# Chunked attention and four attention experts on one core: one written global order in place of four engine orders played out by a planner

## The chip, the cores and the metric

The kernel runs on one core of a Trainium2 chip. The metric is device microseconds of one launch; before the change the median of three runs is 378.93 us (377.97 to 379.02). The core has five engines with a queue of instructions each: TensorE (PE, matmuls; its weight loads are shown apart as PEld), VectorE (DVE), ScalarE (ACT), GpSimd (POOL) and SyncE (SP, which here only issues DMAs). Each engine works its queue in order; where an instruction needs another engine's result, or a buffer that another engine still reads, it waits and everything behind it on its engine waits with it.

## The reference, cut to what matters

```python
# q, k, v: (8, 8, 576, 64); chunks of 64 tokens
scores = scale * q_c @ k_c^T;  attn = softmax(scores)        # 64 x 64 per chunk and head
x = (attn @ v_c) as (8, 576, 512)                            # heads side by side
logits = x @ w_gate;  topk = two largest of four;  w = softmax over these two
for e in range(4):
    q, k, v = x @ wq[e], x @ wk[e], x @ wv[e]
    a = softmax(causal(scale * q @ k^T))                     # 576 x 576
    out += (e in topk) * w * (a @ v @ wo[e])
```

## The kernel before, in words

The 8 x 576 tokens are 36 groups of 128. `stage_a` does the chunked attention, for one group or two at once: loads of K, Q and V (L358, L359, L362, 256 KB each), QK (matmuls of 64 x 64, L468), row maxima, difference, exponential and sum (DVE L478, L480, L485; ACT L483), scaling on POOL (L496), a transpose (for the first five groups on PE, L369 with copies L505 on ACT; for all others POOL copy L376, DMA transpose L380, ACT copy L385), then the product with V (AV below, L541). Its result x is split in two float32r parts, high (ACT L554) and low (DVE L556). Weights are loaded (L412) and split in the same way (ACT L415, DVE or POOL L419).

For each batch b of 8 follow: projections to Q and K of the experts (`project_qk`, L584, 12 matmuls of 256 or 320 columns), to V and the gate's logits (`project_v`, L441), the gate (`gating`, 16 small POOL operations with two on DVE and one on ACT between), and for each of two pairs of experts `scores` (L679, mask and minimum on DVE L690, exponential on ACT L702), `weights` (scaling on POOL L724, transposes on PE L369 with ACT copies L744 and L748, the tallest block by POOL, DMA and ACT L385) and `values` (L773). `project_out` (L801, six matmuls of 512 columns) makes the output rows, copied by ACT or DVE (L806, L809) and stored by SP.

In the text a step is named by its function, batch and pair: "SC4.1" is `scores` of batch 4, pair 1; TR are the PE transposes of `weights`, VA is `values`, OUT is `project_out`, QK and AV are the two products of `stage_a` with the numbers of their groups.

Each step is added to a `Plan` as an operation with an engine, a duration, the operations it depends on and the buffers (`Slot`) it uses. `ORDER` holds for each engine the order of its operations as a list of numbers. `Plan.emit` plays the program out with the durations, `LAT` and `CHANGE` (the price of a change of matmul form on PE): an operation is written when its engine is free, its turn has come, its operands are there and a buffer is free; the buffer that came free first is taken (`u.t = u.pool.pop(0)`). Where PE had nothing ready before 25 us (`WARM`), the planner writes a warming matmul of 128 x 512 bf16 on the last free PSUM bank (L837); 43 of these stand in the built program, 40 have a record in the trace.

Of the kernel before, what the change touches and what calls it, by code (L numbers as in the profile page):

```python
# [36 lines left out]
def rows(i):  # L37
# [3 lines left out]
TICK = 3.4133  # L41
CHANGE = {("full", "quarters"): 0.158, ("full", "rows"): 0.135, ("full", "cols"): 0.170, ("quarters", "rows"): 0.153, ("quarters", "full"): 0.228,
          ("quarters", "cols"): 0.184, ("rows", "full"): 0.248, ("rows", "quarters"): 0.181, ("rows", "cols"): 0.204,
          ("cols", "full"): 0.205, ("cols", "quarters"): 0.161, ("cols", "rows"): 0.129}


START = {"PE": 0.9, "Pool": 6.0, "ACT": 2.5, "SP": 0.4}


# [11 lines left out]
class Op:  # L61
    __slots__ = ("eng", "dur", "fn", "deps", "uses", "rank", "at", "left", "after", "ready", "share", "form")


class Plan:


    LAT = {("PE", "PE"): 0.0, ("DVE", "ACT"): 0.13, ("ACT", "DVE"): 0.14, ("Pool", "PE"): 0.14, ("Pool", "DVE"): 0.13,
           ("DVE", "DVE"): 0.13, ("ACT", "ACT"): 0.13, ("Pool", "Pool"): 0.13, ("SP", "dma"): 0.0, ("dma", "load"): 2.0,
           ("dma", "turn"): 0.5, ("dma", "store"): 1.3}  # L70
# [4 lines left out]
    def add(self, eng, dur, fn, deps=(), uses=(), share=0.9, form="full"):  # L75

        o = Op()
        o.form = form
        o.eng, o.dur, o.fn, o.uses = eng, dur, fn, list(uses)
        o.deps = [d for d in deps if d is not None]  # L80
        o.share = share
        o.at = len(self.ops)
        o.after, o.ready, o.rank = [], 0.0, 0
        o.left = len(o.deps)
        for d in o.deps:
            d.after.append(o)
        for u in o.uses:
            u.left += 1
        self.ops.append(o)
        return o  # L90

    def emit(self, fill, until):

        free_at, avail = {}, {}
        cols, form, turn = {}, "full", {eng: 0 for eng in ORDER}

        def pe_time(dur, share, now):
            up = cols.get(int(now // TICK) - 1, 0.0) >= 0.375 * TICK
            dur = dur if up else 2.0 * dur
            t = now  # L100
            while t < now + dur - 1e-6:
                k = int(t / TICK + 1e-9)
                e = min(now + dur, (k + 1) * TICK)
                cols[k] = cols.get(k, 0.0) + (e - t) * share * (1.0 if up else 0.5)
                t = e
            return dur

        for eng, text in ORDER.items():
            own = [o for o in self.ops if o.eng == eng]
            for r, k in enumerate(text.split()):  # L110
                own[int(k)].rank = r
        for o in self.ops:
            avail.setdefault(o.eng, [])
            free_at.setdefault(o.eng, START.get(o.eng, 0.0))
            if o.left == 0:
                heapq.heappush(avail[o.eng], (o.rank, o.at, o))
        events = [(t, -1, None) for t in sorted(free_at.values())]
        now, left = 0.0, len(self.ops)
        while left:
            for eng, heap in avail.items():  # L120
                if free_at[eng] > now or not (heap or eng == "PE" and now < until):
                    continue
                back, got = [], None
                while heap:
                    item = heapq.heappop(heap)
                    o = item[2]
                    if o.rank != turn.get(eng, o.rank):
                        back.append(item)
                        break
                    need = {}  # L130
                    for u in o.uses:
                        if u.t is None:
                            need[id(u.pool)] = (u.pool, need.get(id(u.pool), (None, 0))[1] + 1)
                    if o.ready <= now and all(len(p) >= n for p, n in need.values()):
                        got = o
                        break
                    back.append(item)
                for item in back:
                    heapq.heappush(heap, item)
                if got is None:  # L140
                    if eng == "PE" and now < until:
                        fill()
                        free_at[eng] = now + pe_time(0.215, 1.0, now)
                        heapq.heappush(events, (free_at[eng], -1, None))
                    continue
                for u in got.uses:
                    if u.t is None:
                        u.t = u.pool.pop(0)
                got.fn()
                left -= 1  # L150
                dur = got.dur
                if eng == "PE":
                    dur = pe_time(dur + CHANGE.get((form, got.form), 0.0), got.share, now)
                    form = got.form
                if eng in turn:
                    turn[eng] += 1
                free_at[eng] = now + dur
                heapq.heappush(events, (now + dur, got.at, got))
            if not left:
                return max(free_at.values())  # L160
            assert events, "the plan is stuck"
            now = events[0][0] + 1e-9
            while events and events[0][0] <= now:
                o = heapq.heappop(events)[2]
                if o is None:
                    continue
                for u in o.uses:
                    u.left -= 1
                    if u.left == 0:
                        u.pool.append(u.t)  # L170
                for a in o.after:
                    a.left -= 1
                    a.ready = max(a.ready, now + self.LAT.get((o.eng, a.eng), 0.21))
                    if a.left == 0:
                        heapq.heappush(events, (a.ready, -1, None))
                        heapq.heappush(avail[a.eng], (now if a.eng == "dma" else a.rank, a.at, a))
# [10 lines left out]
def pool_t(n):  # L187
# [3 lines left out]
ORDER = {  # L191
    "PE": """
# [10 lines left out]
    """,  # L203
    "DVE": """
# [65 lines left out]
    """,  # L270
}
WARM = 25.0
TALL = (4,)
FIRST = 5
# [7 lines left out]
def chunked_attention_then_attention_experts(ctx: ExitStack, tc: tile.TileContext, qt, kt, vt, wqk, wvg, wo, out):  # L282
    nc = tc.nc
    pe, dve, act, pool = nc.tensor, nc.vector, nc.scalar, nc.gpsimd
# [592 lines left out]
```

## Time and profile before

| what | value |
|---|---|
| median of three runs | 378.93 us (377.97 to 379.02) |
| span of the profiled execution, first to last instruction | 376.5 us, 13435 instructions |
| around the span (median less span) | 2.4 us |
| busy: PE, ACT, DVE, POOL | 368.8, 302.5, 265.7, 245.9 us |
| chain that ended last, by engine | PE 79%, ACT 9%, DVE 3%, POOL 3%, DMA 2%, issue 2% |

The page gives busy times, a strip of 40 slices, the chain of work that ended last and the costliest groups. PE is busy nearly throughout, so an average says little; what counts are the few places where PE's queue stands still, and in the opening what it stands still for. PE's granted clock is shown as full in every slice of the strip. The records of matmuls overlap (they are pipelined), so a step's length is read from the start of its first matmul to the start of the next step's first.

### The profile page before, as it was taken

The numbers are of one execution on the slowest core, as the hardware profiler recorded it, in microseconds if no ns is written. First come the engines' busy times: TensorE is split into PE (matmuls) and PEld (weight loads), VectorE is DVE, ScalarE is ACT, GpSimd is POOL, SyncE is SP. The second block draws the span as 40 slices with busy tenths as digits, with TensorE's granted clock in tenths as the row PEclk, the third lists the DMA queues.
The fourth block names the chain that finished last, engine by engine and source line by source line (L and its number), as shares of the span: only waits on it lengthen the run. The fifth ranks groups of instructions, "written<-read, shape, count | busy, mean of one in ns | idle before, by whom it ended". The sixth has DMA issues, their size and how long they took to land.

```text
span 376.5 us, 13435 instructions
## 1 busy us (share of the span) xinstructions
PE 368.8 (98%) x5214; PEld 315.8 (84%) x5217; DVE 265.7 (71%) x895; ACT 302.5 (80%) x845; POOL 245.9 (65%) x447
## 2 busy tenths in 40 slices
PE   8999999999999999999999989999999999999996
PEld 3699889978889799887899789978898889976775
DVE  3769898679978943589697786867864675388631
ACT  2674899999987996898956989799985895799651
POOL 6571778996898059966774418999693039867700
PEclk9999999999999999999999999999999999999999
DMA  7968788589899803149799394669526002235634
GB/s 281 390 228 269 189 177 240 89 179 157 197 186 204 149 30 92 49 114 269 179 257 226 58 245 137 100 169 156 164 51 113 2 3 56 59 57 96 175 124 167
DMA packets 88624, 57.25 MB, mean 152 GB/s; under 512 B 68976, under 2 KB 69232, under 8 KB 88560
## 3 DMA queue, kind: packets, MB, share of 16 engines
q1 hardware_dynamic: 88416, 56.12, 60.3%
q8 instruction: 41, 0.67, 0.8%
q10 hardware_dynamic: 144, 0.26, 0.2%
q14 instruction: 23, 0.19, 0.2%
HBM read 30.42 MB, written 9.44 MB: 106 GB/s over the span
## 4 chain that ended last, share of the span: by engine, by line
PE 79%; ACT 9%; DVE 3%; POOL 3%; DMA 2%; issue 2%; SPq 0%; POOLq 0%; DVEq 0%; ACTq 0%
PE bank L584 21%; PE bank L801 14%; PE bank L441 11%; PE bank L773 11%; PE bank L679 8%; ACT at L702 5%; PE bank L468 4%; PE bank L369 4%; PE bank L541 4%; PE bank L837 3%; DMA wpT<-wp 1%; POOL at L724 1%; ACT et L385 1%; POOL en L496 1%; DMA qs<-in_qt_dram 1%
## 5 line engine op out<-in xcount | busy, mean ns | idle before, releaser
L724 POOL TENSOR_SCALAR at<-at,st,gate 128x192 f32<-128x192 f32 (+4 forms) x160 | 95.4, 609 | 11.9 <-DVE st L715 4.4
L702 ACT ACTIVATE at<-at,st 128x576 f32<-128x576 f32 (+4 forms) x160 | 89.8, 586 | 4.0 <-DVE st L690 3.8
L584 PE MATMUL bank<-xh,wqk_hi 128*128 128x256 f32 (+1 forms) x256 | 71.6, 302 | 0.0
L584 PE MATMUL bank<-xh,wqk_lo 128*128 128x256 f32 (+1 forms) x256 | 70.0, 296 | 0.0
L690 DVE CUSTOM_DVE_ANT_0 at<-bank,mask 128x320 f32<-128x320 f32 (+4 forms) x160 | 59.9, 422 | 14.0 <-PE bank L679 11.9
L496 POOL TENSOR_TENSOR en<-e,mx 128x512 f32<-128x512 f32 x36 | 37.6, 1058 | 27.1 <-DVE mx L487 24.1
L584 PEld LDWEIGHTS bank<-xh,wqk_hi 128*128 128x128 f32 x256 | 48.3, 189 | 2.3 <-issue 0.5
L584 PEld LDWEIGHTS bank<-xh,wqk_lo 128*128 128x128 f32 x256 | 48.4, 189 | 0.2
L773 PE MATMUL bank<-aT,vv 128*64 128x448 f32 (+4 forms) x384 | 47.0, 393 | 0.0
L584 PE MATMUL bank<-xl,wqk_hi 128*128 128x256 f32 (+1 forms) x256 | 44.5, 296 | 0.0
L773 PEld LDWEIGHTS bank<-aT,vv 128*64 128x64 f32 x384 | 24.6, 137 | 22.4 <-issue 15.7
L756 DVE STREAM_TRANSPOSE aT<-at 32x96 f32<-32x96 f32 x128 | 34.4, 269 | 11.7 <-POOL wp L376 3.7
L385 ACT ACTIVATE et<-wpT 128x1024 uint16<-128x1024 uint16 x31 | 36.9, 1192 | 6.1 <-DMA wpT<-wp 6.0
L748 ACT ACTIVATE aT<-bank 128x128 f32<-128x128 f32 (+1 forms) x160 | 37.2, 338 | 3.7 <-PE bank L369 3.5
L385 ACT ACTIVATE aT<-wpT 128x1024 uint16<-128x1024 uint16 x32 | 38.1, 1198 | 1.0 <-DMA wpT<-wp 0.8
L584 PEld LDWEIGHTS bank<-xl,wqk_hi 128*128 128x128 f32 x256 | 37.7, 189 | 0.0
L702 ACT ACTIVATION_READ_ACCUMULATOR at<-at,st 128x1 f32 (+1 forms) x160 | 35.9, 224 | 0.0
L376 POOL COPY wp<-at 128x1024 uint16<-128x1024 uint16 x32 | 32.8, 1036 | 1.0 <-DMA wpT<-wp 0.8
L441 PE MATMUL bank<-wvg_hi,xh 128*128 128x260 f32 x128 | 33.0, 289 | 0.0
L376 POOL COPY wp<-en 128x1024 uint16<-128x1024 uint16 x31 | 31.7, 1039 | 1.6 <-DMA wpT<-wp 1.3
L679 PE MATMUL bank<-kh,qh 64*128 64x288 f32 (+4 forms) x192 | 32.4, 325 | 0.1
L441 PE MATMUL bank<-wvg_lo,xh 128*128 128x260 f32 x128 | 32.2, 283 | 0.0
(104 smaller groups left out, 868.7 us busy)
## 6 DMA issues: line engine op xcount, KB each, us to landing
ks<-in_kt_dram SPq DMA_DIRECT2D x36, 256.0 KB, 4.3
vs<-in_vt_dram SPq DMA_DIRECT2D x36, 256.0 KB, 4.5
qs<-in_qt_dram SPq DMA_DIRECT2D x35, 256.0 KB, 4.6
out_dram<-y SPq DMA_DIRECT2D x35, 256.0 KB, 2.1
at<-in_wqk_dram SPq DMA_DIRECT2D x4, 256.0 KB, 6.5
wpT<-wp SPq DMA_TRANSPOSE x63, 3.4
at<-in_wvg_dram SPq DMA_DIRECT2D x2, 260.0 KB, 4.9
at<-in_wo_dram SPq DMA_DIRECT2D x2, 256.0 KB, 6.0
```

The lines of the kernel that those rows point to most:

```text
L376: pool.tensor_copy(p.t[:, :256 * n].rearrange("p (x n) -> p x n", x=2), src().bitcast(U16).rearrange("p (n x) -> p x n", x=2))
L385: act.activation(put().bitcast(U16).rearrange("p j (q x) -> p j q x", x=2), pt.t[:, :256 * n].rearrange("p (x j q) -> p j q x", x=2, j=n), ...
L441: pe.matmul(bk.t[0:rows, :W_VG], xp[:, k, cols], wp[:, k, :], start=(n == 0), stop=(n == 3 * KT - 1))
L496: pool.tensor_tensor(en.t.rearrange("p (s h k) -> p s h k", s=2, h=HP), ev, rv.to_broadcast([128, 2, HP, 64]), op=OP.mult)
L584: pe.matmul(bk.t[:, :c1 - c0], wp[:, k], xp[:, k, c0:c1], start=(n == 0), stop=(n == 3 * KT - 1))
L679: pe.matmul(bks[s].t[:rows(i), at:at + c1 - c0], q[own, cs], k[own, c0:c1], start=(x == 0), stop=(x == 2), skip_group_check=True)
L690: dve.tensor_tensor_reduce(out=a.t[:r, A_OFF[i] + c0:A_OFF[i] + c1], in0=bk.t[:r, at:at + w], in1=mask[:r, m0:m0 + w], scale=1.0, scalar=f ...
L702: act.activation(af, af, AF.Exp, scale=-1.0, bias=st.t[:r, 0, i, 0:1], accum_out=st.t[:r, 1, i, 0:1])
L724: pool.tensor_scalar(af, af, st.t[:r, 2, i, 0:1], gt.t[:r, i, e:e + 1], op0=OP.mult, op1=OP.mult)
L748: act.activation(dst, bk.t[:, s0:s0 + 64 * n].rearrange("p (j c) -> p j c", j=n), AF.Copy)
L773: pe.matmul(bk.t[64 * s:64 * s + 64, c0 - h0:h1 - h0], vs.t[:, j, 64 * (2 * pair + s):64 * (2 * pair + s) + 64], ts[s].t[:, 448 * j + c0:4 ...
L801: pe.matmul(bk.t[:, n0:n1], up[:, k, 128 * t:128 * t + 128], wp[:, k, n0:n1], start=(n == 0), stop=(n == 5), skip_group_check=True)
```

## The change

The same 2457 operations with the same matmuls, transfers and vector instructions are written in another order. `ORDER` is now one list over all engines; each number is an operation, and `w48` means eight warming matmuls into bank 4. `HOMES` gives the buffer number of each `Slot` in the order of the operations. `emit` no longer plays anything out: it writes the operations in the order of the list. The warming matmuls are 30 (8, 2, 15, 1 and 4, in five places) where the built program had 43.

```diff
-    def emit(self, fill, until):
-        free_at, avail = {}, {}
-        cols, form, turn = {}, "full", {eng: 0 for eng in ORDER}
...
-                if got is None:
-                    if eng == "PE" and now < until:
-                        fill()
-                        free_at[eng] = now + pe_time(0.215, 1.0, now)
...
-                for u in got.uses:
-                    if u.t is None:
-                        u.t = u.pool.pop(0)
-                got.fn()
...
+    def emit(self, fill):
+        homes = iter("".join(HOMES.split()))
         for o in self.ops:
+            for u in o.uses:
+                if u.t is None:
+                    u.home = int(next(homes))
+                    u.t = u.pool[u.home]
+        held, done = {}, set()
...
+        for k in ORDER.split():
+            if k[0] == "w":
+                for _ in range(int(k[2:])):
+                    fill(int(k[1]))
+                continue
+            o = self.ops[int(k)]
...
+            o.fn()
+            retire(o)
...
-ORDER = {
-    "PE": """
-3 0 9 4 1 6 2 5 57 61 12 10 7 55 63 53 13 8 11 16 14 58 64 18 60 62 59 73 15 75 76 20 74 56 54 17 68 66 67 65 90 24
...
-WARM = 25.0
+ORDER = """
+63 40 278 86 109 w48 69 66 20 70 25 72 w42 46 71 43 73 35 47 74 132 49 48 50 170 75 51 76 89 52 77 10 53 5 54 15 w615
...
-    plan.emit(lambda: banks and pe.matmul(banks[-1], warm[:, 0:128], warm, start=True, stop=True), WARM)
+    plan.emit(lambda i: pe.matmul(banks[i], warm[:, 0:128], warm, start=True, stop=True))
```

Three places of the built order follow; in the new one line numbers are lower by 50 from the function `load` on.

The first is SP's queue at the start of the program, before: ks and qs hold K and Q of a group, vs its V, and at a raw half of a weight.

```order
1 L358 DMA ks0_73<-in_kt_dram 128x512
2 L359 DMA qs0_69<-in_qt_dram 128x512
3 L412 DMA at0_107<-in_wvg_dram 128x520
4 L358 DMA ks1_74<-in_kt_dram 128x512
5 L358 DMA ks2_75<-in_kt_dram 128x512
6 L359 DMA qs2_71<-in_qt_dram 128x512
7 L358 DMA ks3_76<-in_kt_dram 128x512
8 L359 DMA qs3_72<-in_qt_dram 128x512
9 L362 DMA vs0_77<-in_vt_dram 128x512
10 L412 DMA at0_107<-in_wvg_dram 128x520
11 L362 DMA vs1_78<-in_vt_dram 128x512
12 L362 DMA vs2_79<-in_vt_dram 128x512
```

And the same stretch of SP's queue now.

```order
1 L308 DMA ks0_73<-in_kt_dram 128x512
2 L309 DMA qs0_69<-in_qt_dram 128x512
3 L308 DMA ks1_74<-in_kt_dram 128x512
4 L312 DMA vs0_77<-in_vt_dram 128x512
5 L308 DMA ks2_75<-in_kt_dram 128x512
6 L309 DMA qs2_71<-in_qt_dram 128x512
7 L308 DMA ks3_76<-in_kt_dram 128x512
8 L309 DMA qs3_72<-in_qt_dram 128x512
9 L312 DMA vs1_78<-in_vt_dram 128x512
10 L362 DMA at0_107<-in_wvg_dram 128x520 x2
11 L312 DMA vs2_79<-in_vt_dram 128x512
12 L362 DMA at1_108<-in_wo_dram 128x512
```

The second group's K (ks1) stands one place earlier, the V weights' first half seven places later with the second half behind it, and the load in fourth place is now the V of group 11, which is used much later.

The second place is POOL's queue in the gate of batch 1, before: gs and gw are the gate's scratch, wp the operand of a DMA transpose, en the scaled weights of `stage_a`.

```order
114 L496 TENSOR_TENSOR en_84<-e_81,mx_91 128x512
115 L376 COPY wp_114<-en_84 128x1024
116 L376 COPY wp_115<-at_108 128x1024
117 L376 COPY wp_113<-at_107 128x1024
118 L640 TENSOR_TENSOR gs_129<-gs_129 128x20
119 L641 TENSOR_TENSOR gs_129<-gs_129 128x5x2
120 L642 TENSOR_TENSOR gs_129<-gs_129 128x5
121 L643 TENSOR_SCALAR gs_129<-gs_129 128x5
122 L648 TENSOR_TENSOR gs_129<-gs_129 128x20
123 L649 COPY gate_127<-gs_129 64x16
```

And POOL's queue at the same gate now.

```order
113 L446 TENSOR_TENSOR en_84<-e_82,mx_92 128x512
114 L590 TENSOR_TENSOR gs_129<-gs_129 128x20
115 L591 TENSOR_TENSOR gs_129<-gs_129 128x5x2
116 L592 TENSOR_TENSOR gs_129<-gs_129 128x5
117 L593 TENSOR_SCALAR gs_129<-gs_129 128x5
118 L326 COPY wp_114<-en_84 128x1024
119 L326 COPY wp_115<-at_109 128x1024
120 L326 COPY wp_113<-at_107 128x1024
121 L598 TENSOR_TENSOR gs_129<-gs_129 128x20
122 L599 COPY gate_127<-gs_129 64x16
```

The sum (L643, now L593) and the scaling (L648, now L598) have a reciprocal on DVE between them; three copies now stand in that place instead of ahead of it.

The third place is PE ahead of the third group that two batches share (its `project_v` reads xch), before: the last products of SC4.1, then QK31, eight rows of two.

```order
1845 L679 MATMUL bank_62<-kh_102,ql_100 128x320
1846 L679 MATMUL bank_66<-kh_102,ql_100 128x320
1847 L468 MATMUL bank_61<-ks_73,qs_69 64x64 x2
1848 L468 MATMUL bank_64<-ks_73,qs_69 64x64 x2
1849 L468 MATMUL bank_61<-ks_73,qs_69 64x64 x2
1850 L468 MATMUL bank_64<-ks_73,qs_69 64x64 x2
```

And PE at that `project_v` now: the last products of AV23+24 run straight into it.

```order
1783 L491 MATMUL bank_62<-et_86,vs_79 64x64 x2
1784 L491 MATMUL bank_65<-et_86,vs_79 64x64 x2
1785 L391 MATMUL bank_66<-wvg_hi,xch_89 128x260
1786 L391 MATMUL bank_66<-wvg_lo,xch_89 128x260
1787 L391 MATMUL bank_66<-wvg_hi,xch_89 128x260
```

QK29+30 and QK31 have left the run AV25+26, AV23+24, QK29+30, SC4.1, QK31 and now stand ten steps later, behind a `project_qk` of batch 5.

## Rows read from the trace of the kernel before

**Rows 1.** The page's first part: busy us, share of the span, instructions.
```profile
PE 368.8 (98%) x5214; PEld 315.8 (84%) x5217; DVE 265.7 (71%) x895; ACT 302.5 (80%) x845; POOL 245.9 (65%) x447
```
**Rows 2.** Stretches: us, busy (x count) of PE, PEld, DVE, ACT, POOL; clock, DMA share, GB/s.
```profile
10.00:20.00 10.00, 9.68 (x184) 7.01 (x184) 7.65 (x21) 6.37 (x17) 6.14 (x6) 1.00 1.05 388
...
60.00:90.00 30.00, 29.75 (x468) 26.88 (x466) 23.03 (x80) 28.75 (x80) 26.00 (x48) 1.00 0.82 168
90.00:110.00 20.00, 19.98 (x319) 17.57 (x317) 17.21 (x56) 19.40 (x54) 18.66 (x27) 1.00 0.78 187
110.00:200.00 90.00, 89.99 (x1290) 77.42 (x1287) 66.86 (x227) 74.98 (x208) 59.95 (x103) 1.00 0.64 153
```
**Rows 3.** Timeline of PE, opening: start, us, engine, line, operation, count [idle before].
```profile
1.25 4.27 PE L837 MATMUL bank<-warm 128*128 128x512 bf16 x10 [1.25 <-DVE warm L319]
...
7.89 3.84 PE L837 MATMUL bank<-warm 128*128 128x512 bf16 x16
...
14.77 1.24 PE L541 MATMUL bank<-et,vs 64*64 64x64 f32 x64
16.17 1.46 PE L837 MATMUL bank<-warm 128*128 128x512 bf16 x6 [0.16 <-issue]
17.27 0.47 PE L441 MATMUL bank<-wvg_hi,xh 128*128 128x260 f32 x1
```
**Rows 4.** Timeline of SP's DMA issues, opening.
```profile
8.31 0.33 SPq L362 DMA_DIRECT2D vs<-in_vt_dram  x1
9.00 0.33 SPq L412 DMA_DIRECT2D at<-in_wqk_dram  x1
```
**Rows 5.** Timelines of DVE, ACT and POOL, opening.
```profile
8.02 0.76 DVE L478 TENSOR_REDUCE mx<-bank 128x4 f32<-128x256 f32 x2 [0.42 <-PE bank L468]
...
11.04 0.64 ACT L415 ACTIVATE wvg_hi<-at 128x520 fp32r<-128x520 f32 x1 [0.94 <-DMA at<-in_wvg_dram]
...
10.42 2.05 POOL L496 TENSOR_TENSOR en<-e,mx 128x512 f32<-128x512 f32 x2 [2.38 <-DVE mx L487]
```
**Rows 6.** DMA queues, whole span, then 211.9 to 224.3 us: packets, MB, share.
```profile
q8 instruction: 41, 0.67, 0.8%
...
q8 instruction: 1, 0.02, 0.5%
```
**Rows 7.** Timeline of PE around 219.55 us.
```profile
215.63 2.10 PE L541 MATMUL bank<-et,vs 64*64 64x64 f32 x128
217.54 1.11 PE L468 MATMUL bank<-ks,qs 64*64 64x64 f32 x64
...
219.55 0.32 PE L468 MATMUL bank<-ks,qs 64*64 64x64 f32 x2
221.20 0.69 PE L468 MATMUL bank<-ks,qs 64*64 64x64 f32 x30 [1.32 <-issue]
```
**Rows 8.** Timeline of PE, two waits for ACT's copies.
```profile
85.94 1.15 PE L541 MATMUL bank<-et,vs 64*64 64x64 f32 x60 [0.19 <-ACT aT L748]
...
345.95 0.50 PE L801 MATMUL bank<-wo_hi,uh 128*128 128x512 f32 x1 [0.61 <-ACT aT L748]
```
**Rows 9.** Timelines: POOL and PE at TR0, POOL at the gate, ACT and PE at VA0.1.
```profile
64.67 3.46 POOL L724 TENSOR_SCALAR at<-at,st,gate 128x192 f32<-128x192 f32 x6
69.69 1.09 PE L369 MATMUL bank<-ident,at 64*128 64x64 f32 x28
...
88.41 0.23 POOL L648 TENSOR_TENSOR gs<-gs 128x20 f32<-128x20 f32 x1 [2.56 <-DVE st L715]
...
92.40 1.16 ACT L385 ACTIVATE aT<-wpT 128x1024 uint16<-128x1024 uint16 x1
94.45 1.94 PE L773 MATMUL bank<-aT,vv 128*64 128x128 f32 x12
```
**Rows 10.** The chain that ended last, in order of time: start, us, what.
```profile
167.76 1.09 PE bank L468 x64
168.85 0.93 PE bank L541 x64
```

More of the change, by code (lines that the diff above doesn't have):

```diff
@@ L1 @@
 from contextlib import ExitStack
-import heapq
 import numpy as np
@@ L38, in rows @@
     return 128 if i else 64
[L41 to L47, printed above, removed]
 class Slot:
@@ L61 @@
 class Op:
-    __slots__ = ("eng", "dur", "fn", "deps", "uses", "rank", "at", "left", "after", "ready", "share", "form")
+    __slots__ = ("eng", "dur", "fn", "deps", "uses", "at", "after", "share", "form")
+NO_CODE = ("dma", "load", "turn", "store")
 class Plan:
-    LAT = {("PE", "PE"): 0.0, ("DVE", "ACT"): 0.13, ("ACT", "DVE"): 0.14, ("Pool", "PE"): 0.14, ("Pool", "DVE"): 0.13,
-           ("DVE", "DVE"): 0.13, ("ACT", "ACT"): 0.13, ("Pool", "Pool"): 0.13, ("SP", "dma"): 0.0, ("dma", "load"): 2.0,
-           ("dma", "turn"): 0.5, ("dma", "store"): 1.3}
     def __init__(self):
@@ L82, in add @@
         o.at = len(self.ops)
-        o.after, o.ready, o.rank = [], 0.0, 0
-        o.left = len(o.deps)
+        o.after = []
         for d in o.deps:
@@ L90, in add @@
         return o
-    def emit(self, fill, until):
-        free_at, avail = {}, {}
-        cols, form, turn = {}, "full", {eng: 0 for eng in ORDER}
[L97 to L111, printed above, removed]
-        for o in self.ops:
[L113 to L131, printed above, removed]
-                        if u.t is None:
[L133 to L139, printed above, removed]
-                if got is None:
-                    if eng == "PE" and now < until:
-                        fill()
-                        free_at[eng] = now + pe_time(0.215, 1.0, now)
-                        heapq.heappush(events, (free_at[eng], -1, None))
-                    continue
-                for u in got.uses:
-                    if u.t is None:
-                        u.t = u.pool.pop(0)
-                got.fn()
[L150 to L176, printed above, removed]
@@ new lines, in emit, with retire @@
+    def emit(self, fill):
+        homes = iter("".join(HOMES.split()))
+        for o in self.ops:
+            for u in o.uses:
[3 more added lines that the diff above has]
+        held, done = {}, set()
+        def retire(o):
+            done.add(o.at)
+            for u in o.uses:
+                u.left -= 1
+            for a in o.after:
+                if a.eng in NO_CODE and all(d.at in done for d in a.deps):
+                    retire(a)
+        for k in ORDER.split():
[4 more added lines that the diff above has]
+            o = self.ops[int(k)]
+            assert all(d.at in done for d in o.deps), "an operation before its operands"
+            for u in o.uses:
+                key = id(u.pool), u.home
+                assert held.get(key, u) is u or held[key].left == 0, "a buffer before it is free"
+                held[key] = u
+            o.fn()
+            retire(o)
+        assert len(done) == len(self.ops)
@@ L188, in pool_t @@
     return 0.24 + 0.833e-3 * n
-ORDER = {
-    "PE": """
[10 rows of a table removed]
-    """,
-    "DVE": """
[20 rows of a table removed]
-    """,
-    "ACT": """
[23 rows of a table removed]
-    """,
-    "Pool": """
[10 rows of a table removed]
-    """,
-    "SP": """
[6 rows of a table removed]
-    """,
-}
-WARM = 25.0
+ORDER = """
+63 40 278 86 109 w48 69 66 20 70 25 72 w42 46 71 43 73 35 47 74 132 49 48 50 170 75 51 76 89 52 77 10 53 5 54 15 w615
+115 23 30 78 118 207 28 116 24 55 119 92 80 117 0 57 56 93 164 29 38 95 w41 58 120 94 96 61 112 121 39 59 79 60 97 w04
[81 rows of a table added]
+"""
+HOMES = """
+3201112231111015700010100006741223231313712333245020265160012300017476003012221130511100003117100133232021222010020221
+0034513032210114600003315400122201007111016111311710000100022171020011122250332113521301021320461130012511021111203603
+3300002020302121157222410010024200501223332411310020120143300011000120203206022033112111302022047022211015130020111153
+0033402000212003013312233500020213204711000261110110100263406400101001557521233401436101141000605200021637152100032221
+7361140205271237365410073214133223675010007112607064012007152301201311201262311140703053654050616411413324576050111540
+2163520200162617310203202417512014230205765402151363261233700714101165200236370120274635101135110637311001120271014273
+6000562141332720661101110206360450120522730101123027427424140407177565061200244331136105271011512062200422007235040121
+4702152102406111016105317370403466413312005270121671012632622000173541002511070512020622241071520614052330331152461701
+21270272070722002470150121411035535071411202
+"""
 TALL = (4,)
```

149 rows, old and new, of the table ORDER are left out of this document.

## The prediction

> **What bounds the kernel now.** I read the busy times first, then the busy times by stretch, then the timeline of each engine where PE stands still. The reader is to see in the first that PE is busy for 368.8 of 376.5 us and no other engine for more than 302.5 [rows 1]: a new order can win only what PE stands still, plus what its own queue holds that isn't needed. The stretches say where that is. From 110 to 200 us PE is busy 89.99 of 90 us [rows 2], so nothing is to be had there. In the opening PE looks busy too (9.68 of 10 us between 10 and 20), but much of it is warming: ten warming matmuls from 1.25, sixteen from 7.89, six from 16.17, and the first projection only at 17.27 [rows 3]. In that stretch the DMA engines are full (share 1.05, 388 GB/s) [rows 2], SP's issues follow each other at 0.69 us (8.31 to 9.00) [rows 4], and a load of 256 KB at 388 GB/s takes 0.68 us. So the opening is bound by the sequence of loads and the chain DVE, ACT, POOL behind them, and PE fills it.
>
> Between 60 and 110 us a second engine is nearly full beside PE: ACT 28.75 of 30 and 19.40 of 20 us, POOL 18.66 of the last 20 [rows 2]. There PE's lead is small: the transposes TR0 start at 69.69 where POOL has finished their operands at 68.13, and VA0.1 starts at 94.45 where ACT's last copy for it ends at 93.56 [rows 9]. Later both have more room, and PE waits in only two visible places: 1.32 us inside QK31 [rows 7] and 0.61 us at 345.95 [rows 8].
>
> **The change part by part.** The sum is made against the profiled execution: a span of 376.5 us, and 2.4 us around it up to the median of 378.93.
>
> *The work itself.* Same matmuls, transfers and vector instructions. What differs on PE is how often its form changes (full, quarters, rows, columns): counted over the order without the warming matmuls 107 before, 109 now. A change costs 0.16 us: 64 matmuls of `stage_a` take 1.09 us behind another form and 0.93 behind their own [rows 10]. Two more are +0.3 us.
>
> *The warming matmuls.* Thirteen fewer than the 43 that were written. At full clock one is 0.22 to 0.24 us (16 in 3.84, six in 1.46), in the first 4.27 us 0.43 (ten) [rows 3]. Thirteen times 0.22 is 2.8 us of PE's queue, but they stood where PE waited anyway, so alone their removal is worth nothing; what counts is when the first projection can start.
>
> *The opening.* The chain to that projection goes: QK of groups 1 and 0, maxima and differences on DVE, exponential, sum, scaling on POOL, transpose, copy, AV, split of x, projection. Group 0's K is loaded one place earlier, which is 0.68 us; its first reduction on DVE at 8.02 had waited 0.42 for QK [rows 5] and now follows group 1's at once, so POOL's two scalings (10.42 to 12.47) [rows 5] and the transposes come some 0.4 us earlier. Both halves of the V weights now come at the place where the second stood; the second was split on ACT from 11.04 [rows 5], so the two are split from 11.0 to 12.3, and POOL's remainders (1.29 each) end at 14.7, ahead of need. ACT then copies group 0's transposes first and group 1's second half only after group 0's x is split. By these lengths AV0 starts at about 13.5 instead of 14.77 and the projection at 16.3 instead of 17.27. Against that the V of group 11 now stands fourth among the loads and puts all behind it 0.68 us back; that is in the times named. Behind the projection both orders run the same first steps; a wait of 0.3 us before a transpose at 26 us goes too. I take -1.0 us; bounds +0.7 (the load that isn't needed yet costs its whole length) and -2.8 (all thirteen matmuls).
>
> *The wait inside QK31.* PE stops at 219.87 after two of 32 matmuls of a step that has begun, so its operands are there; the profile shows no releaser ("issue") [rows 7]. One queue carries instructions in 41 transfers of 0.67 MB together [rows 6]; over PE's 5214 matmuls and 5217 weight loads [rows 1] that is 64 bytes each, so it is PE's program, about 256 instructions to a transfer. Between 211.9 and 224.3 us only one such transfer ran [rows 6], while PE worked off its densest run: 128 matmuls of AV from 215.63, 64 of QK, 12 of SC4.1 and two of QK31 [rows 7], each with its weight load, 412 instructions in 4.2 us. I read the wait as PE running out of program. The new order takes QK29+30 and QK31 out of that run. Counting in blocks of 256 from the start, PE before needed 3.3 us for the 320 instructions up to the place where it stopped and 4.3 or more at every other block; in the new order the least is 4.6. From the step's start to its resumption are 1.65 us, of which two matmuls and the change of form take about 0.15: I take -1.5 us; bounds 0 and -1.6.
>
> The Trainium skill, "Runtime: NRT & Kernel Launch", section "Instruction fetch mechanics", says that PE's program is fetched ahead in blocks of 256 instructions and that this is hidden, since dispatch is slower than the fetch. The block size agrees with the 0.67 MB in 41 transfers; that it is always hidden doesn't agree with the wait at 219.87, unless that has another cause. By the page this term would be 0 and the sum 1.5 us worse.
>
> *Waits on ACT between 85 and 90 us, at 120 and at 345.* At 85.94 AV11+12 stops after four matmuls for ACT's copies, and at 345.95 the first OUT of batch 5 waits 0.61 us [rows 8]. Measured from a step's first matmul to the next step's first, against the same steps elsewhere, these two cost 0.5 and 0.7 us, and two late starts of `scores` at 89 and 120 us cost 0.6 and 0.4: 2.2 us together. The new order puts AV11+12 behind SC1.1, and an OUT that is long ready between the transposes of batch 7. In the gate of batch 1 POOL had stood 2.56 us for a reciprocal on DVE [rows 9]; three copies now cover it, which gives the transposes of batch 1 more room. But in the same stretch ACT and POOL stay as full as they were. If PE comes to TR0 1.6 us earlier (0.6 by its place, 1.0 by the opening), POOL, whose operations up to there are the same in number and which finished 1.56 us ahead, must be earlier too. I take half, -1.1 us, bounds -2.2 and +2.
>
> *The end.* From VA7.1 on both orders hold the same steps, with one OUT more between VA7.1 and the last batch's; the last copies and stores are the same: 0, bounds -0.5 and +0.5.
>
> Sum: 0.3 - 1.0 - 1.5 - 1.1 + 0 = -3.3. With 376.5 and 2.4 this is 375.6; I say 375.8, since the opening's steps are the least sure.
>
> **The rivals.** *ACT and POOL take the lead back.* If they set the times from TR0 to VA1.0, what PE wins before 90 us is lost there, and only the refill and the wait at 345 remain: 0.3 - 1.5 - 0.6, or 377.1. For it speaks that ACT is at 96% there [rows 2]; against it that ACT's work ahead of VA0.1 is 1.5 us less in the new order, and that POOL's 2.56 us go.
>
> *The refill wait stays or moves.* In the new opening AV2, AV3, a transpose, QK5+6, QK7+8 and AV4 follow each other: 232 matmuls, in a stretch where the DMA engines are full. By its place between two transfers PE has 4.9 us there, against 3.3 where it stopped, but a transfer may be slower beside the loads. Then 1.5 us stay: 377.3.
>
> *Slower: transposes brought too near their scores.* Between the end of the `scores` of a pair and its first transpose lies a chain over DVE, ACT, DVE and POOL. In PE's own work the shortest such distance before was 15.1 us outside the last batch (batch 3, pair 0). Now it is 12.7 there, 15.4 instead of 18.0 at the first pair, and 16.4 and 20.7 instead of 31 and 36 at two others. If the chain needs what it had at the first two places, PE waits 2.4 + 2.6 = 5.0 us: 380.8. It decides from 4.3 us of such waits on. For it: ACT's 96%. Against it: 13.4 us was enough in batch 7, with no wait before its transposes, and from 110 us on ACT is busy 74.98 of 90 us only [rows 2].
>
> *The clock.* With fewer warming matmuls PE stands still in short pieces before 16 us. Its granted clock is full in all rows of the stretches. If it fell to 1.2 GHz and came back only some 4 us into the projections, they would take twice as long there, as the first warming matmuls do (0.43 against 0.22) [rows 3]: +4, or 379.8. No piece without work is longer than about 1 us by the times above, so I hold it for unlikely.
>
> **How the numbers follow.** Forecast 0.48, ACT and POOL 0.20, refill 0.12, transposes 0.10, clock 0.03, and 0.07 for more than forecast (all waits go and none comes: about 372.5). A measurement can't tell less than 0.3% (1.1 us: 377.8 to 380.1) from no change. The forecast ends below that nearly always; the second and third in two cases of three; the transposes and half of the clock cases lie above. That gives faster 0.72, same 0.16, slower 0.12. The forecast's own range is 373.6 to 377.5; the range over the cases is 372.9 to 379.0, with the transposes left out at its upper end.
>
> **What would show it.** The first `project_v` at about 16.3 us; the DMA share near 1 up to 24 us as before; no "issue" wait of over 1 us on PE; TR0 and VA0.1 1 to 2 us earlier than 69.69 and 94.45; POOL's first scaling at the gate of batch 1 without the wait of 2.56 us; the span 373 to 374 us. The forecast is wrong if PE waits for POOL or ACT at TR0, TR3 or VA0.1 by more than a microsecond, if a wait without releaser of that size stands at 24 to 28 us, or if the granted clock falls in the opening.

## The result, and the profile after

The changed kernel takes 383.04 us (median of 4 runs, 381.85 to 383.76), beside 378.51 us before (377.97 to 379.02): ratio 1.0111, interval 1.0078 to 1.0145. It is slower, where 375.8 was forecast.

The first part of the page after: busy us, share of the span (380.7 us), instructions.

```profile
PE 369.7 (97%) x5202; PEld 316.6 (83%) x5204; DVE 265.5 (70%) x895; ACT 301.4 (79%) x845; POOL 245.6 (65%) x447
```

Beside [rows 1] PE is busy 0.9 us longer, DVE, ACT and POOL a little less, and the span is 4.2 us longer. The chain that ended last does look different, before first, then after:

```profile
PE 79%; ACT 9%; DVE 3%; POOL 3%; DMA 2%; issue 2%; SPq 0%; POOLq 0%; DVEq 0%; ACTq 0%
```

```profile
PE 53%; DMA 14%; ACT 13%; POOL 8%; DVE 5%; issue 4%; SPq 2%; POOLq 0%; ACTq 0%; DVEq 0%
PE bank L534 13%; DMA wpT<-wp 12%; PE bank L751 10%; PE bank L391 8%; PE bank L723 8%; PE bank L629 6%; ACT at L652 4%; POOL at L674 4%; PE bank L418 3%; PE bank L491 3%; PE bank L319 2%; ACT aT L335 2%; POOL wp L326 2%; DMA qs<-in_qt_dram 2%; DVE at L640 2%
```

12% of the span, 46 us, now hangs on one kind of transfer, the transposes by DMA (wp to wpT). The stretches of [rows 2], after (line numbers after are 50 lower than before):

```profile
10.00:20.00 10.00, 8.82 (x217) 6.71 (x216) 7.69 (x22) 7.21 (x18) 8.45 (x8) 1.00 1.05 387
60.00:90.00 30.00, 29.23 (x407) 26.24 (x407) 23.16 (x78) 28.29 (x82) 25.71 (x46) 1.00 0.78 156
90.00:110.00 20.00, 19.97 (x395) 17.51 (x393) 15.50 (x54) 17.90 (x53) 14.48 (x20) 1.00 0.77 160
110.00:200.00 90.00, 87.26 (x1248) 74.93 (x1239) 66.59 (x222) 74.25 (x206) 59.77 (x104) 1.00 0.66 155
```

Where PE was busy 89.99 of 90 us before, it is busy 87.26. The clock is full in every stretch. Three places of PE's timeline answer to [rows 3, 7]: the first projection, QK7+8 and QK31.

```profile
16.41 0.39 PE L391 MATMUL bank<-wvg_hi,xh 128*128 128x260 f32 x1
...
26.98 1.09 PE L418 MATMUL bank<-ks,qs 64*64 64x64 f32 x59 [0.29 <-issue]
...
233.97 1.63 PE L418 MATMUL bank<-ks,qs 64*64 64x64 f32 x96
```

The projection starts 0.86 us earlier, and QK31 runs through. So what the change was read to bring is there. What it cost stands in the groups of instructions by line (busy, mean ns, idle time before them and its releaser), the two kinds of copies of transposed blocks, before and after:

```profile
L385 ACT ACTIVATE aT<-wpT 128x1024 uint16<-128x1024 uint16 x32 | 38.1, 1198 | 1.0 <-DMA wpT<-wp 0.8
...
L385 ACT ACTIVATE et<-wpT 128x1024 uint16<-128x1024 uint16 x31 | 36.9, 1192 | 6.1 <-DMA wpT<-wp 6.0
```

```profile
L335 ACT ACTIVATE aT<-wpT 128x1024 uint16<-128x1024 uint16 x32 | 38.4, 1208 | 6.4 <-DMA wpT<-wp 6.3
...
L335 ACT ACTIVATE et<-wpT 128x1024 uint16<-128x1024 uint16 x31 | 36.6, 1183 | 13.2 <-DMA wpT<-wp 13.0
```

ACT stands 19.3 us before such copies instead of 6.8. How that reaches PE is seen around 120 us, on ACT's timeline and then on PE's:

```profile
119.96 1.17 ACT L335 ACTIVATE aT<-wpT 128x1024 uint16<-128x1024 uint16 x1 [0.49 <-DMA wpT<-wp]
121.04 0.37 ACT L401 ACTIVATE vv<-bank 128x260 f32<-128x260 f32 x1
121.31 1.17 ACT L335 ACTIVATE aT<-wpT 128x1024 uint16<-128x1024 uint16 x1
122.37 0.38 ACT L401 ACTIVATE vv<-bank 128x260 f32<-128x260 f32 x1
```

```profile
120.97 0.40 PE L629 MATMUL bank<-kl,qh 64*128 64x288 f32 x2 [0.60 <-DVE kl L548]
...
122.80 0.24 PE L629 MATMUL bank<-kh,qh 64*64 64x64 f32 x1 [0.84 <-ACT vv L401]
```

The scores at 122.80 need a PSUM bank that a projection of V filled earlier. Its copy into vv (122.37) was ready, but stood on ACT behind two copies of transposed blocks (119.96, 121.31), the first waiting for its transfer. All eight banks are taken there. The row names vv; the cause stands two places ahead of it in ACT's queue.

From the first projection on, each step's length (first weight load to the next step's first) is compared with the lower quartile of like steps (same kind, same form of the next step); what is over counts as standing still:

| | before | after |
|---|---|---|
| first projection at | 17.25 | 16.41 |
| work of the steps | 343.27 | 344.04 |
| standing still | 11.53 | 15.73 |
| of it in QK31 (before), QK7+8 (after) | 1.64 | 0.52 |
| last step at | 372.05 | 376.18 |

Without those two stops, standing still grew from 9.9 to 15.2 us; 6.0 us of growth lies between 40 and 200 us, in a dozen waits of 0.3 to 1.0 us and smaller ones.

### The profile page after: what moved, and what is told of

Its sections match the earlier page's. It is cut to its first block, busy times and chain, and to the rows that moved or that the text cites. A ratio compares the mean times of both kernels' runs of the same rounds, so it can differ in the third digit from the quotient of the medians.

```text
span 380.7 us, 13403 instructions
## 1 busy us (share of the span) xinstructions
PE 369.7 (97%) x5202; PEld 316.6 (83%) x5204; DVE 265.5 (70%) x895; ACT 301.4 (79%) x845; POOL 245.6 (65%) x447
## 4 chain that ended last, share of the span: by engine, by line
PE 53%; DMA 14%; ACT 13%; POOL 8%; DVE 5%; issue 4%; SPq 2%; POOLq 0%; ACTq 0%; DVEq 0%
PE bank L534 13%; DMA wpT<-wp 12%; PE bank L751 10%; PE bank L391 8%; PE bank L723 8%; PE bank L629 6%; ACT at L652 4%; POOL at L674 4%; PE bank L418 3%; PE bank L491 3%; PE bank L319 2%; ACT aT L335 2%; POOL wp L326 2%; DMA qs<-in_qt_dram 2%; DVE at L640 2%
## 5 line engine op out<-in xcount | busy, mean ns | idle before, releaser
L674 POOL TENSOR_SCALAR at<-at,st,gate 128x448 f32<-128x448 f32 (+4 forms) x160 | 95.3, 611 | 18.0 <-DVE st L665 7.3
L534 PE MATMUL bank<-xh,wqk_hi 128*128 128x320 f32 (+1 forms) x256 | 71.8, 302 | 0.5 <-DVE st L640 0.5
L534 PE MATMUL bank<-xh,wqk_lo 128*128 128x320 f32 (+1 forms) x256 | 70.0, 296 | 0.0
L534 PE MATMUL bank<-xl,wqk_hi 128*128 128x320 f32 (+1 forms) x256 | 44.5, 296 | 0.0
L629 PE MATMUL bank<-kh,qh 64*128 64x288 f32 (+4 forms) x192 | 34.2, 326 | 2.1 <-ACT vv L401 0.8
L652 ACT ACTIVATION_READ_ACCUMULATOR at<-at,st 128x1 f32 (+1 forms) x160 | 32.9, 206 | 0.0
```

Of the source, the lines that this page charges most:

```text
L534: pe.matmul(bk.t[:, :c1 - c0], wp[:, k], xp[:, k, c0:c1], start=(n == 0), stop=(n == 3 * KT - 1))
L629: pe.matmul(bks[s].t[:rows(i), at:at + c1 - c0], q[own, cs], k[own, c0:c1], start=(x == 0), stop=(x == 2), skip_group_check=True)
L652: act.activation(af, af, AF.Exp, scale=-1.0, bias=st.t[:r, 0, i, 0:1], accum_out=st.t[:r, 1, i, 0:1])
L674: pool.tensor_scalar(af, af, st.t[:r, 2, i, 0:1], gt.t[:r, i, e:e + 1], op0=OP.mult, op1=OP.mult)
```

## The experiments

Each was timed beside the kernel before, which took 378.2 to 378.6 us. Times are medians, the ratio is to before, with its interval. Differences to the changed kernel are to its 383.04 us; its own interval (1.0078 to 1.0145) is 2.5 us wide, so a difference to it of a microsecond or two is at the edge of what can be told. Orders are shown by rows of the engine's program.

**Ready work passes waiting copies (ACT alone).** One place of 16:

```diff
+L401 ACTIVATE vv_105<-bank_65 128x260
+L401 ACTIVATE vv_105<-bank_66 128x260
 L335 ACTIVATE aT_112<-wpT_117 128x4x256
-L401 ACTIVATE vv_105<-bank_65 128x260
 L335 ACTIVATE aT_111<-wpT_116 128x4x256
-L401 ACTIVATE vv_105<-bank_66 128x260
```

> The changed kernel with one edit: on ACT, 40 operations that were ready by the trace pass 16 copies of DMA-transposed blocks that still waited for their transfer; the other four engines' orders and all buffers stay. Theory A (ACT stands before such copies, 19 us in the changed kernel against 7 before, 11 us of it with ready work behind, and PE then waits for PSUM banks whose last readers are in that work): most of the 4.5 us comes back, 379.3 us (378.3 to 380.8). Theory B (the fixed banks): no change, 383.0. Theory C (PE's own order brings steps too near to each other, whatever ACT does): 382 to 383.5.

381.23 us, 1.0085 (1.0071 to 1.0099): 1.8 of the 4.5 us. Its copies still waited 10.2 us, and the chain moved back to PE:

```profile
PE 81%; DMA 7%; ACT 4%; POOL 3%; issue 2%; DVE 1%; SPq 1%; ACTq 0%; DVEq 0%; POOLq 0%
```

Theory A has the sign by the medians (the intervals overlap), not the size.

**Other banks, same order.** Only the table of buffers differs (351 of 988 entries).

> The changed kernel with the same order on every engine, but each PSUM bank chosen anew: at every step the bank that by the trace had come free longest ago (351 of the 988 buffer choices differ). Theory A (copies ahead of ready work on ACT) and theory C (PE's order): 383.0 us, 382.3 to 383.8, since by the trace all eight banks are taken at the stalls and the longest free one is as late as the chosen one. Theory B (fixed banks make PE wait for one that is late while another is free): 379 to 381 us.

384.85 us, 1.0168 (1.0142 to 1.0194). Theory B falls: nothing is won. That it is 1.8 us above the changed kernel neither theory had; the two intervals just touch, and whether the banks cost something stays open.

**The new opening alone, behind it the old order.** The list is the new one up to AV2 at 23.8 us, then the old one without what has run.

> The new opening alone: all that the changed kernel issues up to the first AV step of group 2 (23.8 us), 30 warming matmuls with it, and behind it everything else in the order of the kernel before, written as one list. If the opening's gain of 0.9 us by the two traces stays: 377.5 us (377.0 to 378.0). If ACT and POOL take it back at 60 to 110 us (the prediction's first rival): 378.4. If writing the order as one list with fixed buffers costs by itself: above 379.5.

377.35 us, 0.9981 (0.9966 to 0.9995). The opening's gain stays, and the written list costs nothing by itself.

**The dense run taken apart, in the old order.** PE's steps:

```diff
 AV25+26  AV23+24
-QK29+30
 SC4.1a  QK31  PVcut2
+QK29+30
```

> The kernel before, written as one list, with one step moved: the scores of groups 29 and 30 (64 small matmuls) stand behind the cut projection instead of ahead of SC4.1a and QK31, so that the dense run in which PE stood 1.32 us is 64 matmuls shorter. If that wait is PE running out of program and goes: 377.2 us (376.9 to 377.8), 1.5 less and two changes of form of 0.16 more. If the wait is something else or only moves: 378.5 to 378.9.

377.6 us, 0.9989 (0.9978 to 1.0): 0.6 us, at the edge of what can be told. In its trace the stop is gone. The orders of the other engines are those of before, but 387 of the 988 buffers differ as well, so the 0.6 us are not the step's move alone.

**A second pass on ACT.** The first edit's trace, treated alike, copies that are ready but not urgent included.

> The first edit (381.2 us) taken a step further, on ACT alone again: by that run's own trace 60 more operations pass 23 copies of transposed blocks, those that still wait for their transfer, and those that are ready but not needed by PE for 3 us while a PSUM bank waits to be copied. If what is left of the loss is still ACT taking such copies ahead of bank copies (by the trace at 48.6, 121.6 and 337 us, 0.98, 1.16 and 1.32 us): 379.5 us (379.0 to 380.3). If the first edit took all that this mechanism costs and the rest is PE's order: 381 to 381.8.

384.6 us, 1.0163 (1.0146 to 1.018). Missed: what the first edit gained is given back, and more. PE's large waits now lie at TR0.1 (0.8 and 0.9 us), SC1.1 (0.9), SC2.1 (1.5), TR5.1 (1.2) and AV34+35 (1.3). My reading is that blocks copied later make the next steps late, so that the room is too small on both sides; it isn't shown, as the rows there name copies out of banks and DVE, not these blocks.

**Less to load, in both kernels.**

```diff
-            nc.sync.dma_start(k_s[g].t, kt[g])
+            n = HP if len(filled) < 8 else 1
+            filled.update((id(k_s[g].t), id(q_s[g].t)))
+            nc.sync.dma_start(k_s[g].t[:, :n], kt[g][:, :n])
...
```

> The changed kernel with less to load: once each of the four buffers of Q, of K and of V has been filled, every further load brings only the first quarter of its block (the output is that of partly old blocks). All instructions stay; the transposes by DMA meet less traffic. If the loss is transfers that land later than the new order allows for: 379 to 380.5 us, and the difference to the same cut in the kernel before shrinks from 4.7 to 2 or less. If transfers play no part (banks, PE's order): 382 to 383.

> The kernel before with the same cut of its loads, as the partner of the run above. Its copies waited 7 us for transfers where the changed kernel's waited 19, and PE's large stops had other reasons: 377.5 to 378.3 us by either theory.

After: 376.7 us, 0.9959 (0.9936 to 0.9982), 6.3 less. Before: 377.42 us, 0.9972 (0.9963 to 0.998). With less traffic the new order is not slower than the old. More came back than I expected: ACT's waits for transposes only fell from 19.3 to 12.3 us, and the load that came late for QK27+28 (0.6 us) is in time too. How the rest divides wasn't taken apart. The DMA issues of the thin changed kernel (KB, median us from issue to landing; 4.3 to 4.9 us for full loads):

```profile
ks<-in_kt_dram SPq DMA_DIRECT2D x32, 64.0 KB, 2.1
qs<-in_qt_dram SPq DMA_DIRECT2D x32, 64.0 KB, 2.4
...
wpT<-wp SPq DMA_TRANSPOSE x63, 3.3
```

**Copies that wait for no transfer, in both kernels.**

```diff
+    still = sb.tile([128, 1024], U16, name="still")
+    dve.memset(still, 0)
...
-                           pt.t[:, :256 * n].rearrange("p (x j q) -> p j q x", x=2, j=n), AF.Copy)
+                           still[:, :256 * n].rearrange("p (x j q) -> p j q x", x=2, j=n), AF.Copy)
```

> The changed kernel, in which ACT's 63 copies of transposed blocks read one block of zeros that stands still in SBUF instead of the block that the DMA engines write (the output leaves the transposed values out). All loads and transposes are still issued, in the same order, but nothing waits for a transpose to land. If late transposes are the way by which transfers cost the changed kernel its time: 377 us (376 to 378.3), as with the thin loads. If the loads themselves land late at the scores of stage a: 381 to 383.

> The kernel before with the same edit. Its copies waited 6.6 us in all, at places where PE mostly had a lead: 377.3 to 378.3 us. A gain above 1.5 us here would mean that the edit takes away more than those waits.

After: 376.41 us, 0.9949 (0.993 to 0.9968). Before: 378.06 us, 0.9996 (0.9982 to 1.001). The same edit is worth 6.6 us in the new order and nothing that can be told in the old one. All transposes and loads still run, in the same order; ACT's waits for the transposes are gone. With them goes SP's wait for the buffers that the copies read (4.2 us in the changed kernel, 2.6 before). The copies and the chain in the changed kernel so edited (its lines stand 2 lower in the file):

```profile
L337 ACT ACTIVATE aT<-still 128x1024 uint16<-128x1024 uint16 x32 | 38.4, 1207 | 0.0
L337 ACT ACTIVATE et<-still 128x1024 uint16<-128x1024 uint16 x31 | 36.6, 1183 | 0.0
```

```profile
PE 80%; ACT 9%; DMA 7%; DVE 1%; issue 1%; POOL 1%; SPq 1%; POOLq 0%; ACTq 0%; DVEq 0%
```

The loss is shown to go through these waits. SP's earlier issues are hardly where the gain comes from: what they could bring sooner to PE are loads, and PE waits for loads longer than in the changed kernel, 2.2 us instead of 0.6, at QK23+24 and QK27+28:

```profile
171.57 0.69 PE L420 MATMUL bank<-ks,qs 64*64 64x64 f32 x32 [1.47 <-DMA qs<-in_qt_dram]
...
189.87 0.69 PE L420 MATMUL bank<-ks,qs 64*64 64x64 f32 x32 [0.71 <-DMA qs<-in_qt_dram]
```

So the new order is tight at its loads too; behind the late copies this was hardly seen.

**Only one kind of copy freed, changed kernel.** `still` is read where the copy goes into et, or where it goes into aT.

> The changed kernel, where only the 31 copies of stage a (into et) read the standing zeros; the 32 copies into aT wait for their transposes as written (the transposed values of stage a are left out of the output). In the changed kernel the former waited 13.0 us and the latter 6.3 us. If the cost is ACT standing still in order, whoever it waits for, the 6.6 us divide about as these waits: 378.5 us (377.5 to 379.7). If the cost sits with the operands of the values (aT) alone: 381.5 to 383.

> The partner: only the 32 copies into aT read the standing zeros. In-order waiting on ACT: a third of the gain, 380.8 us (379.7 to 381.9). Operands of the values alone: 376.5 to 378.

et: 380.21 us, 1.0049 (1.0031 to 1.0066). aT: 379.55 us, 1.0028 (1.0014 to 1.0043). Gains of 2.8 and 3.5 us, together 6.3; which of the two is larger can't be told. Both kinds carry, but not as their waits: 13.0 us of waits into et were worth 2.8, 6.3 us into aT 3.5. One reason is seen in the trace with et freed, where the waits into aT grow from 6.3 to 10.0 us:

```profile
L337 ACT ACTIVATE aT<-wpT 128x1024 uint16<-128x1024 uint16 x32 | 38.4, 1201 | 10.2 <-DMA wpT<-wp 10.0
```

In-order waiting holds for both; that a microsecond of it costs more or less by what is queued behind is my reading. The rival (aT alone) falls.

**Copies brought forward in the old order.** One place of 29:

```diff
+L335 ACTIVATE et_85<-wpT_118 128x1024
 L652 ACTIVATE at_109,st_121<-at_109,st_121 128x320
 L652 ACTIVATE at_107,st_119<-at_107,st_119 128x320
...
-L335 ACTIVATE et_85<-wpT_118 128x1024
```

> The kernel before, written as one list, with 29 of ACT's copies of transposed blocks moved ahead of 2 to 24 other ACT operations each, so that by its own trace ACT comes to them 0.3 to 1.0 us before the block has landed, 20 us in sum beside the 6.6 us it had. Everything that needs these blocks gets them earlier, nothing else moves. If standing before such copies is what costs (by what is queued behind them), it is slower like the changed kernel: 381.5 us (380 to 384). If the cost in the changed kernel came from blocks that PE needs and gets late, this one gains or stays: 377.5 to 378.5.

417.99 us, 1.1002 (1.0958 to 1.1045). The sign is as expected, the size is not: 39 us where 3 were expected. The waits rose to 32.3 us, PE's standing still to 48.7.

```profile
L335 ACT ACTIVATE aT<-wpT 128x1024 uint16<-128x1024 uint16 x32 | 38.0, 1191 | 11.1 <-DMA wpT<-wp 10.1 <-PE bank L751 1.0
...
L335 ACT ACTIVATE et<-wpT 128x1024 uint16<-128x1024 uint16 x31 | 36.4, 1179 | 22.2 <-DMA wpT<-wp 22.2
```

Part of this is TensorE's clock, full in the traces before and after. Here the granted clock stood at 0.50 (1.2 instead of 2.4 GHz) in five stretches, each beginning about where a stop of PE of 1.7 to 3.0 us ends. For the first of them, the end of the stop on PE's timeline, then the stretch (columns as in [rows 2]):

```profile
94.21 0.40 PE L629 MATMUL bank<-kh,qh 64*128 64x288 f32 x1 [2.00 <-ACT aT L698]
```

```profile
94.90:101.60 6.70, 6.17 (x39) 5.89 (x40) 5.00 (x22) 4.29 (x10) 5.49 (x12) 0.50 0.28 92
```

The five are 20 us together, so I estimate the clock's part at 10 of the 39 us; it is in the 48.7 too. Each copy moved also puts its own 1.2 us ahead of what it passes; how the rest divides between that and the waits wasn't taken apart. But every one of these blocks was taken as early as it could be, and the kernel became slower: an early block alone doesn't help.

**Loads behind the transposes (SP alone).** 41 loads change places with the transpose that follows:

```diff
-L308 DMA ks_75<-in_kt_dram 128x512
-L309 DMA qs_71<-in_qt_dram 128x512
 L330 DMA_TRANSPOSE wpT_118<-wp_115 128x8x128
+L308 DMA ks_75<-in_kt_dram 128x512
+L309 DMA qs_71<-in_qt_dram 128x512
```

> The changed kernel with one edit on SP alone: 41 loads of K, Q and V that were issued less than 4.5 us ahead of a transpose, 10 to 120 us before PE uses them, are issued right behind that transpose. By the trace a transpose takes 2.8 us from issue to landing with under 20 KB of other traffic beside it, and 4.4 us with 400 KB or more (20 of 63 in the changed kernel, 13 before). If it is this meeting that makes the transposes late: 379.5 us (378.0 to 381.0). If the time between issue and copy is too short whatever the loads do, or the loads then meet the next transposes: 382 to 383.5.

> The SP edit and the first ACT edit (40 operations past 16 waiting copies, 381.2 us alone) together. If both work on the same waits: 378.5 us (377.5 to 380), less than the sum of the two gains. If the loads behind the transposes do nothing: 381.2.

384.65 us, 1.0182 (1.0156 to 1.0208), and 383.88 us, 1.0147 (1.0124 to 1.017). Missed. In the first run the transposes did get quicker (mean of 3.14 instead of 3.43 us from issue to landing), but a load put behind one transpose stands ahead of the next, and PE waited for a copied block directly:

```profile
93.28 1.99 PE L723 MATMUL bank<-aT,vv 128*64 128x448 f32 x10 [2.60 <-ACT aT L335]
```

The second run has the same stop (2.36 us). So moving loads by this rule is no cure; how far the moved loads made this block late wasn't taken apart.

**What paid, put together.** New opening, old order, dense run apart.

> The two parts of the change that paid, together: the new opening up to 23.8 us with 30 warming matmuls, then the order of before, with the scores of groups 29 and 30 behind the cut projection. If the two gains (0.87 and 0.62 us) add: 376.7 us (376.2 to 377.2). If the opening's run had already taken part of the second (its stop in QK31 is 0.5 instead of 1.6 us): 377.2.

376.51 us, 0.9951 (0.9939 to 0.9963): faster than both kernels, by the two terms of the sum that held.

## Why the prediction was wrong

*The work itself* (+0.3): measured +0.8 in the table. The changes of form were counted right in number, but not by kind: an OUT takes 1.28 us ahead of its own form and 1.6 ahead of scores, which is more than the 0.16 of [rows 10].

*The opening* (-1.0): right, -0.86 by the trace, -0.87 alone on the chip (0.2 to 1.3 by its interval). That the two agree so closely is luck: over the traces kept, the first projection starts at 15.66 to 17.61 us with this opening (eleven runs) and at 17.27 to 18.34 with the old one (five). *Warming matmuls* (0): right as far as seen.

*The wait inside QK31* (-1.5): it went, but a stop of 0.5 us came in QK7+8 at 26.4 us, where the second rival had put it, and alone the edit gave 0.6 on the chip. That the stop belongs to the dense run is borne out; that PE ran out of program there is still a reading. The size was that of one execution: the same instructions in the old order, loads full, stopped 0.62 us in the run with standing copies (last section).

*Waits on ACT* (-1.1, "I take half", bounds -2.2 and +2): this step failed. Standing still outside the two stops grew by 5.3 us, beyond both bounds; in its place stand ACT's waits for transposes (19.3 instead of 6.8 us), whose removal gave 6.6 us back. I looked at PE's visible waits and asked which go; I read 110 to 200 us, PE busy 89.99 of 90, as a stretch where "nothing is to be had", and did not ask how much room the old order held there. The room can be counted from the trace: for each of the 63 copies, the time from the issue of its transpose to the end of the ACT operation ahead of the copy. Before, 13 of 63 had less than 4 us, after 24, while a transpose takes 3.2 (before) to 3.4 us (after) on average and up to 6.9. (The limit matters: under 3.5 us it is 8 and 10.) I wrote "same matmuls, transfers and vector instructions" and let transfers rest there.

*The rivals.* The first (ACT and POOL take the lead back) named the engine, but by its load: ACT is busy 301.4 us, less than before. The third, slower at 380.8, put the danger between scores and PE's transposes; PE waits for none of those by more than 0.3 us (TR0 at 68.47 instead of 69.69). The same question, asked of the transposes by DMA, would have found it. The clock stayed full.

*The signs named.* First projection, DMA share, no long "issue" stop and TR0 came as said, and POOL's 2.56 us at the gate [rows 9] went. The sign against it was put at TR0, TR3 and VA0.1; the waits came at the scores instead, which take two banks in each step.

*The end* (0): right, 4.5 us from the last step to the end in both.

## What to carry to other kernels

An order that fits the lengths of steps can fit them too closely: before a reordering is costed, list for every consumer of a transfer the room from issue to use, and set it beside the spread of that transfer's time, not its mean. On an engine that works in order, ask of each operation that may wait what stands behind it; a full PE in the old profile says that this room was there, not that it isn't needed. A row of waits names the last releaser; where that had been ready long before, look for what stood ahead of it in its queue.

## What the runs showed of the hardware

Transposes by DMA take longer beside loads: by the packets of the trace after, a transpose took 2.8 us from issue to landing with less than 20 KB of other traffic beside it, and 4.4 us with 400 KB or more (20 of 63; 13 before). A longer transfer also meets more, so this alone proves little; but with thin loads the page's median fell from 3.7 to 3.3 us. The Trainium skill, "DMA: Bandwidth & Descriptors", section "Issuing engines are not separate DMA queues", says that DMAs run on the same 16 engines and interleave whoever starts them; the trace agrees as to the interleaving, while nearly all transfers here are started by SP alone. The Trainium skill, "Advanced Engine Details and Errata", section "X-Bar Transpose (TRN2)", call transposes as fast as regular DMAs; here a block of 256 KB moved in 1.4 us (median from first to last packet, both kernels), where a load of that size takes 0.68 us at 388 GB/s [rows 2, 4] and a plain transfer of that size that meets no other takes 0.82 us by its packets.

PE's stop in QK31 differs from execution to execution. The same instructions stop 1.32 us in the kernel before [rows 7]; in the old order with standing copies (loads full, lines 2 higher in number), then with thin loads (lines 8 higher):

```profile
220.58 0.69 PE L470 MATMUL bank<-ks,qs 64*64 64x64 f32 x30 [0.62 <-issue]
```

```profile
219.70 0.33 PE L476 MATMUL bank<-ks,qs 64*64 64x64 f32 x2
220.22 0.69 PE L476 MATMUL bank<-ks,qs 64*64 64x64 f32 x30 [0.20 <-issue]
```

With the new opening ahead of the old order and full loads it is 0.21 us (there after 14 matmuls), so that the other traffic sets its size is not shown.

TensorE's granted clock fell to half at the end of some stops of PE of 1.7 to 3.0 us (copies brought forward, 0.50 from 94.90 to 101.60 us among others), and after the stop of 2.36 us in the second run with moved loads (0.50 from 94.40 to 97.60); after the 2.60 us of the first it stayed at 1.00. So a stop of this size can cost more than its own length.
